# An FNet block with a gated MLP: a second scratch tile, two more tiles of statistics on VectorE, one load earlier, and the first products in another order

## The chip, the cores and the metric

The kernel runs on one core of one Trainium2 chip. The metric is the device time of one execution in microseconds (us). A core has five engines with an instruction queue each: TensorE (PE in the profile, its weight loads PEld), VectorE (DVE), ScalarE (ACT), GpSimd (POOL) and SyncE (SP, which here only issues DMAs). Each queue runs in order, and engines wait for each other through semaphores.

## The reference

```python
x = A_x                                              # 2048 x 512
mod = (silu(c) @ w_mod).reshape(1, 6, 1, 512)
sa, ca, ga, sb, cb, gb = mod[:, 0], ..., mod[:, 5]
h = layernorm(x) * (1 + ca) + sa
a = h @ dft_hid_re.T;  b = h @ dft_hid_im.T          # 512 x 512 each
x = x + ga * (dft_seq_re @ a - dft_seq_im @ b)       # 2048 x 2048 each
h = layernorm(x) * (1 + cb) + sb
z = gelu(h @ w_in);  z1, z2 = z[:, :896], layernorm(z[:, 896:])
g = w_sp @ z2 + b_sp[:, None]                        # w_sp 2048 x 2048
out = x + gb * ((z1 * g) @ w_out)
```

All in float32.

## The kernel before, in words

Every float32 product is made of three products in a faster format: a matrix is split into a rounded part (`..h`, a copy by ScalarE) and the rest (`..l`, a subtraction by VectorE), and `matmul3` adds hi x hi, lo x hi and hi x lo. A product of 128 x 128 by 128 x 512 is one matrix instruction.

Part A is computed with the sequence transform first: G = Cr h and Ci h, then G times the hidden matrices (`ht`). The sequence matrices come in *stages* of 512 x 512 (1 MB, four DMAs of 256 KB on SP's queue, two stage tiles). A stage is four *chunks* n of 128 rows. For a chunk, VectorE transposes 32 x 32 squares from the stage (`t`), ScalarE makes `ah` of it and VectorE `al`; TensorE then does 12 products, `gp` (four blocks k of h's columns, three products each). In the first quarter (t = 0, n = 0 to 31) chunks of Cr and Ci come in turn, four by four: chunks 0 to 3 and 8 to 11 are Cr, 4 to 7 and 12 to 15 are Ci, so that row tile s of x is first needed at chunk 0, 1, 2, 3, 8, 9 and so on: 16 tiles of 128 rows, `x0` to `x3` being the loads of four tiles each.

For a row tile s the normalized tile `xn` is split into `hh` and `hl`. Tiles 0 to 7 have their mean and variance from VectorE (`stats_x`: two small instructions, then a chain of three on POOL, `mvx`, `rsx`, `nmrx`). Tiles 8 to 15 have them from ScalarE: `sum_x`, then `square_x`, with POOL's small steps between (`sums`), each a pass over the tile. `norm_x` then applies them on ScalarE, and column 0 of the tile is set to 1 (by ScalarE for the first four tiles, by POOL for the others): the kernel folds the modulation (1 + ca, sa) into the hidden matrices instead, and needs its two rows of `mod` as columns over the partitions. For those, w_mod's blocks (`wb1`, `wb0`, 1 MB each) are transposed in squares by VectorE into a scratch tile `wt`, multiplied by silu(c) spread over the partitions (`crow`), and summed along the row by ScalarE into one column of `col1` or `col0`: `weigh_column(j, k)` and `sum_column(j, k)`, eight times. `wt` is one tile.

The order is written by hand. A loop over chunks n (*slots*) calls `prep(n)`, which issues t and ah of chunk n + 3 and al of chunk n + 2, then `mm_a(n)`, the products, then `run(n)`, whatever `at(n, ...)` put down for this slot. A load of x or w_mod that stands in a slot goes to SP's queue at that place; a stage is loaded when the last chunk of the stage before the last has been transposed. Ahead of the first slot, `keep_busy` gives TensorE products of no use (`busyp`) until data arrive.

After 32 chunks the sums are split (`gh`, `gl`), the second quarter follows, and the products with ht (`yp`) of the quarter before, their addition to x, the second norm and the stores stand in its slots. Then come z1, z2, the product with w_sp (`gw`) and with w_out.

Of the kernel before, what the change touches and what calls it, by code (L numbers as in the profile page):

```python
# [19 lines left out]
def fnet_gmlp_kernel(  # L20
# [24 lines left out]
    nc = tc.nc  # L45
    S, D = x.shape[1:]
# [11 lines left out]
    def pool(name, side="left", bufs=1):  # L58
        return tc.tile_pool(name=name, bufs=bufs, side=side, reuse_waits="tile")
# [11 lines left out]
    def bank(k, name):  # L71
        return psum.tile([P, 512], F32, tag=f"bank{k}", bufs=1, name=name)
# [5 lines left out]
    def split(hi, lo, src):  # L78

        nc.scalar.activation(hi, src, AF.Copy)  # L80
        nc.vector.tensor_tensor(lo, src, hi.bitcast(F32), op=ALU.subtract)

    def matmul3(acc, ah, al, bh, bl, first, last):
        nc.tensor.matmul(acc, ah, bh, start=first, stop=False)  # L84
        nc.tensor.matmul(acc, ah, bl, start=False, stop=False)  # L85
        nc.tensor.matmul(acc, al, bh, start=False, stop=last)  # L86
# [20 lines left out]
    def apply(dst, src, scale_shift):  # L107
        nc.scalar.activation(dst, src, AF.Identity, bias=scale_shift[1], scale=scale_shift[0])
# [3 lines left out]
    def at(n, f, *a):  # L112
        fill.setdefault(n, []).append((f, a))
# [14 lines left out]
    N2 = 4 * len(src)  # L128
# [17 lines left out]
    def squares(dst, block, k):  # L146
        nc.vector.transpose(dst.rearrange("p (b i) -> p b i", i=32), block[:, :, 32 * k:32 * k + 32])  # L147
# [36 lines left out]
    rows = p2.enter_context(pool("rows", "right"))  # L184
    s1 = ctx.enter_context(ExitStack())
    spool = s1.enter_context(pool("spool", "right"))
# [7 lines left out]
    ones = cpool.tile([P, P], F32, name="ones")  # L194
# [28 lines left out]
    WB, WT, COL = {}, {}, {}  # L223
# [13 lines left out]
        COL[j] = htpool.tile([P, ND], F32, name=f"col{j}")  # L237

    def weigh_column(j, k):
        WT[j, k] = spool.tile([P, D], F32, tag="wt", bufs=1, name=f"wt{j}_{k}")  # L240
        squares(WT[j, k], WB[j], k)
        nc.vector.tensor_tensor(WT[j, k], WT[j, k], WB["c"], op=ALU.mult)

# [11 lines left out]
    def keep_busy(n, k):  # L255

        ps = bank(k, "busyp")
        for _ in range(n):
            nc.tensor.matmul(ps, ones, busy, start=True, stop=True)
# [14 lines left out]
    X, XG, LN, NRM, h_hi, h_lo = {}, {}, {}, {}, {}, {}  # L274

    def load_x(g, ks=range(4)):

        if g not in XG:
            XG[g] = spool.tile([P, 4, D], F32, tag="x", bufs=2, name=f"x{g}")
        k0, k1 = ks[0], ks[-1] + 1  # L280
        v = x.rearrange("(g a k i) d -> g a i k d", g=NQ, a=4, i=32)
        for a in range(4):
            nc.sync.dma_start(XG[g][32 * a:32 * a + 32, k0:k1, :], v[g, a][:, k0:k1, :])
        for k in ks:
            X[4 * g + k] = XG[g][:, k, :]
# [17 lines left out]
        NRM[s] = m[:, 2:3], m[:, 3:4]  # L303

    def norm_x(s):
        if s not in LN:
            LN[s] = spool.tile([P, D], F32, tag="xn", bufs=4, name=f"xn{s}")
        apply(LN[s], X.pop(s), NRM.pop(s))
        if s < 4:
            nc.scalar.activation(LN[s][:, 0:1], ones[:, 0:1], AF.Copy)  # L310
        else:
            nc.gpsimd.memset(LN[s][:, 0:1], 1.0)

    def parts_h(s, t):

# [13 lines left out]
    GP, gt_hi, gt_lo, YP = {}, {}, {}, {}  # L329
# [3 lines left out]
    def mm_a(n):  # L333
        t, r = divmod(n, 8 * NQ)
        j, s = ((r // 4) % 2, r // 8 * 4 + r % 4) if t == 0 else (r // NS, r % NS)
        if s == 0:
            for k in range(ND):
                GP[t, j, k] = bank(4 * j + k if t == 0 else ring[0] % 6, f"gp{t}_{j}_{k}")
                ring[0] += t > 0
        ah, al = AH.pop(n), AL.pop(n)  # L340
        for k in range(ND):
            matmul3(GP[t, j, k], h_hi[s][:, k, :], h_lo[s][:, k, :], ah, al, s == 0, s == NS - 1)
        if s == NS - 1:
            for k in range(ND):
                ps = GP.pop((t, j, k))
                gt_hi[t, j, k] = GP_[0].tile([P, Q], F32R, tag=f"gh{j}_{k}", name=f"gh{t}_{j}_{k}")
                gt_lo[t, j, k] = GP_[0].tile([P, Q], F32R, tag=f"gl{j}_{k}", name=f"gl{t}_{j}_{k}")
                split(gt_hi[t, j, k], gt_lo[t, j, k], ps)
# [261 lines left out]
    load_x(0, range(2, 4))  # L610
    load(1)
    load_x(1, range(2))
    keep_busy(7, 5)
    for s in range(2):
        stats_x(s)
    for s in range(2):
        norm_x(s)
# [7 lines left out]
    lo_h(1)  # L625
    prep_lo(1)
    norm_x(2)
    prep_hi(2)
    stats_x(3)
    hi_h(2)  # L630
    norm_x(3)
    at(0, lo_h, 2)
    at(0, hi_h, 3)
# [3 lines left out]
    at(9, silu_row)  # L637
    at(4, load_x, 2)
    at(5, load_columns, 1)
    at(8, load_columns, 0)  # L640
    at(12, load_x, 3)
    at(19, load_ht, 0)
    at(28, load_ht, 1)
    for s, n in ((4, 4), (5, 4), (6, 6), (7, 6)):
        at(n, stats_x, s)
        at(n + 1, norm_x, s)
        at(n + 2, hi_h, s)
        at(n + 3, lo_h, s)
    for s, n in zip(range(8, NS), (10, 11, 12, 13, 18, 19, 20, 21)):
        at(n, sum_x, s)  # L650
        at(n + 1, square_x, s)
        at(n + 2, norm_x, s)
        at(n + 3, hi_h, s)
        at(n + 4, lo_h, s)
    for j, ns in ((1, (12, 13, 16, 18)), (0, (19, 20, 21, 23))):
        for k, n in enumerate(ns):
            at(n, weigh_column, j, k)
            at(n + 1, sum_column, j, k)
# [6 lines left out]
    ones_r = htpool.tile([P, P], F32R, name="ones_r")  # L665
    at(24, nc.scalar.activation, ones_r, ones, AF.Copy)
    at(26, change_pools)
    for j, turn, weigh, row, fold, hi in ((0, (24, 25, 26, 27), (29, 29, 30, 30), 25, (34, 34, 35, 36), (38, 35, 36, 37)),
                                          (1, (33, 38, 39, 40), (39, 40, 41, 41), 37, (44, 45, 46, 47), (48, 46, 47, 48))):
        for k in range(ND):  # L670
            at(turn[k], turn_ht, j, k)
            at(weigh[k], weigh_ht, j, k)
            at(fold[k], fold_ht, j, k)
        at(row, scale_w0, j)
        at(row + 1, store_w0, j)
        at(row + 5, load_w0, j)
# [14 lines left out]
    for t in range(NQ):  # L691
        n = 8 * NQ * (t + 1)
        for i in range(4):
            y = N2 - 1 if t == NQ - 1 else (54, 56, 58, 60)[i] if t == 0 else n + (8, 10, 12, 14)[i] if t == 1 else n + 1 + 3 * i
            if i < 2:
                at(y - 4, load_xr, t, i)
            if t == 0:
                at((41, 42, 43, 45)[i], mm_y, t, i, (0,))
                at((42, 43, 44, 46)[i], keep_y, t, i)
            at(y, mm_y, t, i, (0, 1) if t else (1,))  # L700
            if t < NQ - 1:
                at(y + 1, post_y, t, i)
                at(y + 2, norm_y, t, i)
                at(y + 3 if t else 71 + i, post_h, t, i)
                if i < 2:
                    at(y + 2 if t else y + 3, load_xr, t, i + 2)
            else:
                if i > 1:
                    at(N2 - 0.25, prep, N2 + i - 2)
                at(N2 - 0.25, post_y, t, i)  # L710
                at(N2 - 0.25, norm_y, t, i)
                at(N2 - 0.25, post_h, t, i)
                if i < 2:
                    at(N2 - 0.25, load_xr, t, i + 2)
# [59 lines left out]
    for t in range(NQ):  # L774
        n = N4 + NS * (t + 1)
# [14 lines left out]
    t = NQ - 1  # L790
# [61 lines left out]
```

## Time and profile before

| | |
|---|---|
| median of 3 runs | 1002.48 us (1002.38 to 1003.36) |
| the profiled execution | 1002.74 us |
| its span in the trace | 1000.9 us |
| granted TensorE clock, mean | 0.997 |
| TensorE busy | 989.3 us (99%), 4346 instructions |
| VectorE, ScalarE, GpSimd busy | 543.6, 315.1, 142.3 us |

All times of a trace count from the span's start. A row of the timeline has the start, the duration, the engine, the line of the code, the operation, what is written from what, and in brackets how long the engine was idle before and whose work ended the wait. A row of the waits has the engine and line that waited, whose work it waited for, the sum in us, how often, and the longest. The granted clock is the share of full speed that TensorE was given.

### The profile page before, as it was taken

What the parts mean: (1) busy time and instruction counts of PE and PEld (TensorE: products, weight loads), DVE (VectorE), ACT (ScalarE), POOL (GpSimd) and SP (SyncE); (2) the same over time, 40 slices, a digit from 0 to 9 for tenths busy, and PEclk for the clock granted to TensorE, in tenths of its full rate; (3) what the DMA queues carried; (4) which work ended last, traced back from release to release, by engine and by line L of the source; (5) the groups of instructions that cost most, each with busy time, mean ns of one, the idle gap of its engine ahead of it and who ended that gap; (6) DMA issues with size and microseconds to landing.
All of it is one profiled execution on the core that took longest, in us unless ns stands there. A gap on an engine that the chain in (4) does not pass through costs nothing.

```text
span 1000.9 us, 11701 instructions
## 1 busy us (share of the span) xinstructions
PE 989.3 (99%) x4346; PEld 818.9 (82%) x4346; DVE 543.6 (54%) x830; ACT 315.1 (31%) x513; POOL 142.3 (14%) x282
## 2 busy tenths in 40 slices
PE   8998999999999999999999999999999999999998
PEld 5886888888878888888888998888888888888886
DVE  6768957775566546547433576555332622262315
ACT  4666423232132312222543665431111111111101
POOL 2321000112420122004321111102000200020002
PEclk9999999999999999999999999999999999999999
DMA  9993852666435443556553232435225222522131
GB/s 214 215 198 67 167 138 63 158 166 171 126 103 118 93 109 104 117 127 163 189 204 117 43 80 47 116 69 147 70 63 156 55 64 64 158 64 52 43 137 43
DMA packets 149466, 115.08 MB, mean 115 GB/s; under 512 B 7200, under 2 KB 130080, under 8 KB 149408
## 3 DMA queue, kind: packets, MB, share of 16 engines
q1 hardware_dynamic: 142576, 93.87, 40.7%
q0 software_dynamic: 6304, 20.46, 5.8%
q8 instruction: 34, 0.56, 0.2%
q14 instruction: 24, 0.20, 0.1%
q10 hardware_dynamic: 528, 0.00, 0.0%
HBM read 94.37 MB, written 19.93 MB: 114 GB/s over the span
## 4 chain that ended last, share of the span: by engine, by line
PE 94%; DVE 2%; ACT 1%; DMA 1%; issue 1%; SPq 0%; DVEq 0%; ACTq 0%
PE gp L85 11%; PE gp L86 11%; PE gp L84 10%; PE gw L84 10%; PE gw L86 10%; PE gw L85 10%; PE yp L85 3%; PE yp L84 3%; PE yp L86 3%; PE z2p L85 3%; PE z2p L84 3%; PE z2p L86 3%; PE z1p L84 3%; PE z1p L85 3%; PE z1p L86 3%; PE op L86 2%
## 5 line engine op out<-in xcount | busy, mean ns | idle before, releaser
L170 ACT ACTIVATE ah<-t 128x512 fp32r<-128x512 f32 x224 | 141.5, 632 | 535.6 <-PE gw L86 214.9
L179 DVE TENSOR_TENSOR al<-t,ah 128x512 fp32r<-128x512 f32 x224 | 153.1, 683 | 274.6 <-PE gw L85 143.0
L85 PE MATMUL gp<-al,hh 128*128 128x512 f32 x512 | 201.6, 394 | 4.7 <-DVE al L179 4.7
L84 PE MATMUL gp<-ah,hh 128*128 128x512 f32 x512 | 200.8, 392 | 1.7 <-ACT ah L170 1.7
L86 PE MATMUL gp<-ah,hl 128*128 128x512 f32 x512 | 201.1, 393 | 0.0
L86 PE MATMUL gw<-ah,zl 128*128 128x512 f32 x448 | 174.5, 390 | 0.0
L84 PE MATMUL gw<-ah,zh 128*128 128x512 f32 x448 | 174.5, 389 | 0.0
L85 PE MATMUL gw<-al,zh 128*128 128x512 f32 x448 | 174.5, 389 | 0.0
L147 DVE STREAM_TRANSPOSE t<-stage 128x512 f32<-128x512 f32 x208 | 146.4, 704 | 5.6 <-DMA stage<-in_A_dft_seq_re_dram 2.8
L85 PEld LDWEIGHTS gp<-al,hh 128*128 128x128 f32 x512 | 96.8, 189 | 26.5 <-DVE al L179 6.3
L84 PEld LDWEIGHTS gp<-ah,hh 128*128 128x128 f32 x512 | 97.0, 189 | 23.2 <-ACT ah L170 2.5
L86 PEld LDWEIGHTS gp<-ah,hl 128*128 128x128 f32 x512 | 97.0, 189 | 20.8 <-DVE hl L325 0.4
L86 PEld LDWEIGHTS gw<-ah,zl 128*128 128x128 f32 x448 | 84.1, 188 | 17.5
L85 PEld LDWEIGHTS gw<-al,zh 128*128 128x128 f32 x448 | 84.2, 188 | 17.4
L84 PEld LDWEIGHTS gw<-ah,zh 128*128 128x128 f32 x448 | 84.1, 188 | 17.3
L569 POOL TENSOR_TENSOR u<-u,g 128x512 f32<-128x512 f32 x16 | 21.4, 1340 | 336.1 <-DVE g L567 336.1
L85 PE MATMUL yp<-htl,gh 128*128 128x512 f32 x128 | 51.1, 399 | 0.0
L84 PE MATMUL yp<-hth,gh 128*128 128x512 f32 x128 | 50.5, 394 | 0.0
L86 PE MATMUL yp<-hth,gl 128*128 128x512 f32 x128 | 50.2, 392 | 0.0
L85 PE MATMUL z2p<-wil,ah 128*128 128x448 f32 x128 | 46.8, 366 | 0.0
L84 PE MATMUL z2p<-wih,ah 128*128 128x448 f32 x128 | 46.8, 366 | 0.0
L86 PE MATMUL z2p<-wih,al 128*128 128x448 f32 x128 | 46.8, 366 | 0.0
(125 smaller groups left out, 1132.0 us busy)
## 6 DMA issues: line engine op xcount, KB each, us to landing
stage<-in_A_dft_seq_re_dram SPq DMA_DIRECT2D x64, 256.0 KB, 4.8
stage<-in_A_dft_seq_im_dram SPq DMA_DIRECT2D x64, 256.0 KB, 4.7
stage<-in_B_w_sp_dram SPq DMA_DIRECT2D x64, 256.0 KB, 4.9
stage<-h_d SPq DMA_DIRECT2D x32, 256.0 KB, 4.6
z_d<-z POOLq DMA_DIRECT2D x28, 256.0 KB, 5.9
u<-z_d SPq DMA_DIRECT2D x4, 1792.0 KB, 7.9
wm<-in_w_mod_dram SPq DMA_DIRECT2D x16, 256.0 KB, 5.7
xr<-in_A_x_dram POOLq DMA_DIRECT2D x16, 256.0 KB, 3.0
```

Of the source, the lines that this page charges most:

```text
L84: nc.tensor.matmul(acc, ah, bh, start=first, stop=False)
L85: nc.tensor.matmul(acc, ah, bl, start=False, stop=False)
L86: nc.tensor.matmul(acc, al, bh, start=False, stop=last)
L147: nc.vector.transpose(dst.rearrange("p (b i) -> p b i", i=32), block[:, :, 32 * k:32 * k + 32])
L170: nc.scalar.activation(AH[n], T[n], AF.Copy)
L179: nc.vector.tensor_tensor(AL[n], T.pop(n), AH[n].bitcast(F32), op=ALU.subtract)
L569: eng.tensor_tensor(U[t][:, f, :], U[t][:, f, :], g, op=ALU.mult)
```

## The change

Four kinds of edits, all in part A's first quarter but one. `weigh_column` takes a second scratch tile for even k, in the place of a row tile ("y") that is not used until later. Row tiles 8 and 9 have their statistics from VectorE instead of ScalarE, and the slots of tiles 8 to 15 and of the columns are set anew; the load of x3 stands in slot 8 and that of wb0 in slot 12. Column 0 of a normalized tile is set by POOL for all tiles, ahead of the norm, which then writes columns 1 to 511. The chunks 0 to 3 have their 12 products in the order hi x hi for the four blocks, lo of the chunk x hi for the four, hi x lo for the four, and there are eight products of no use ahead instead of seven. The one edit outside: the y products of the second quarter (t = 1) stand one slot earlier.

```diff
     def weigh_column(j, k):
-        WT[j, k] = spool.tile([P, D], F32, tag="wt", bufs=1, name=f"wt{j}_{k}")
+        pl, tag = (spool, "wt") if k % 2 else (rows, "y")
+        WT[j, k] = pl.tile([P, D], F32, tag=tag, bufs=1, name=f"wt{j}_{k}")
...
     def norm_x(s):
+
         if s not in LN:
             LN[s] = spool.tile([P, D], F32, tag="xn", bufs=4, name=f"xn{s}")
-        apply(LN[s], X.pop(s), NRM.pop(s))
-        if s < 4:
-            nc.scalar.activation(LN[s][:, 0:1], ones[:, 0:1], AF.Copy)
-        else:
-            nc.gpsimd.memset(LN[s][:, 0:1], 1.0)
+        nc.gpsimd.memset(LN[s][:, 0:1], 1.0)
+        apply(LN[s][:, 1:], X.pop(s)[:, 1:], NRM.pop(s))
...
         ah, al = AH.pop(n), AL.pop(n)
+        if n < 4:
+            for a, b in ((h_hi[s], ah), (h_hi[s], al), (h_lo[s], ah)):
+                for k in range(ND):
+                    nc.tensor.matmul(GP[0, 0, k], a[:, k, :], b, start=s == 0 and b is ah and a is h_hi[s], stop=False)
+            return
         for k in range(ND):
             matmul3(GP[t, j, k], h_hi[s][:, k, :], h_lo[s][:, k, :], ah, al, s == 0, s == NS - 1)
...
-    keep_busy(7, 5)
+    keep_busy(8, 5)
...
-    at(8, load_columns, 0)
-    at(12, load_x, 3)
+    at(8, load_x, 3)
+    at(12, load_columns, 0)
...
-    for s, n in ((4, 4), (5, 4), (6, 6), (7, 6)):
+    for s, n in ((4, 4), (5, 4), (6, 6), (7, 6), (8, 10), (9, 10)):
+        m = n + (s == 9)
         at(n, stats_x, s)
-        at(n + 1, norm_x, s)
...
+        at(m + 1, norm_x, s)
...
-    for s, n in zip(range(8, NS), (10, 11, 12, 13, 18, 19, 20, 21)):
+    for s, n in zip(range(10, NS), (11, 12, 15, 16, 18, 19)):
         at(n, sum_x, s)
...
-    for j, ns in ((1, (12, 13, 16, 18)), (0, (19, 20, 21, 23))):
+    for j, ns in ((1, (12, 14, 17, 18)), (0, (21, 22, 23, 24))):
         for k, n in enumerate(ns):
             at(n, weigh_column, j, k)
             at(n + 1, sum_column, j, k)
...
-    for j, turn, weigh, row, fold, hi in ((0, (24, 25, 26, 27), (29, 29, 30, 30), 25, (34, 34, 35, 36), (38, 35, 36, 37)),
+    for j, turn, weigh, row, fold, hi in ((0, (25, 26, 27, 28), (29, 29, 30, 30), 26, (34, 34, 35, 36), (38, 35, 36, 37)),
...
-            y = N2 - 1 if t == NQ - 1 else (54, 56, 58, 60)[i] if t == 0 else n + (8, 10, 12, 14)[i] if t == 1 else n + 1 + 3 * i
+            y = N2 - 1 if t == NQ - 1 else (54, 56, 58, 60)[i] if t == 0 else n + (7, 9, 11, 13)[i] if t == 1 else n + 1 + 3 * i
```

`sum_x`, `square_x`, `norm_x`, `hi_h` and `lo_h` of a tile stand in slots n to n + 4 as before. Line numbers shift a little: L242 becomes L243, L325 becomes L324, and products of chunks 0 to 3 have L343.

What the order of instructions becomes, at three places. First VectorE at the turns of chunks 24 and 25 (the number after a name's underscore tells buffers apart; `t24` is chunk 24's transpose). Before:

```order
L147 STREAM_TRANSPOSE wt0_1_840<-wb0_486 128x512
L242 TENSOR_TENSOR wt0_1_840<-wt0_1_840,crow_295 128x512
L251 TENSOR_SCALAR col1_388<-col1_388 128x4
L253 TENSOR_SCALAR col2_844<-col1_388 128x4
L147 STREAM_TRANSPOSE t24_846<-stage6_699 128x512
L179 TENSOR_TENSOR al23_850<-t23_806,ah23_808 128x512
L147 STREAM_TRANSPOSE wt0_2_877<-wb0_486 128x512
L242 TENSOR_TENSOR wt0_2_877<-wt0_2_877,crow_295 128x512
L147 STREAM_TRANSPOSE t25_880<-stage6_699 128x512
L179 TENSOR_TENSOR al24_884<-t24_846,ah24_848 128x512
L325 TENSOR_TENSOR hl12_898<-xn12_764,hh12_864 128x512
```

VectorE in the changed kernel, the same chunks:

```order
L252 TENSOR_SCALAR col1_389<-col1_389 128x4
L254 TENSOR_SCALAR col2_866<-col1_389 128x4
L147 STREAM_TRANSPOSE t24_868<-stage6_712 128x512
L179 TENSOR_TENSOR al23_872<-t23_834,ah23_836 128x512
L147 STREAM_TRANSPOSE wt0_0_890<-wb0_603 128x512
L243 TENSOR_TENSOR wt0_0_890<-wt0_0_890,crow_296 128x512
L147 STREAM_TRANSPOSE t25_893<-stage6_712 128x512
L179 TENSOR_TENSOR al24_897<-t24_868,ah24_870 128x512
L324 TENSOR_TENSOR hl14_911<-xn14_790,hh14_886 128x512
```

And ScalarE at the same turns, before:

```order
L170 ACTIVATE ah24_848<-t24_846 128x512
L320 ACTIVATE hh12_864<-xn12_764 128x512
L108 ACTIVATE xn13_798<-x3_590,sums13_799 128x512
L299 ACTIVATE xn14_835,sums14_836<-x3_590,sums14_836 128x512
L294 ACTIVATE xn15_872,sums15_873<-x3_590 128x512
L247 ACTIVATE wt0_1_840,col0_491<-wt0_1_840 128x512
L170 ACTIVATE ah25_882<-t25_880 128x512
L320 ACTIVATE hh13_900<-xn13_798 128x512
```

ScalarE in the changed kernel:

```order
L170 ACTIVATE ah24_870<-t24_868 128x512
L319 ACTIVATE hh14_886<-xn14_790 128x512
L108 ACTIVATE xn15_829<-x3_487,sums15_830 128x511
L170 ACTIVATE ah25_895<-t25_893 128x512
L319 ACTIVATE hh15_913<-xn15_829 128x512
L248 ACTIVATE wt0_0_890,col0_608<-wt0_0_890 128x512
L170 ACTIVATE ah26_921<-t26_919 128x512
L248 ACTIVATE wt0_1_916,col0_608<-wt0_1_916 128x512
```

What moved: at chunk 24 the third weighing of column 0 stood on VectorE, now it is the first, the others follow in the next three slots; on ScalarE the passes over x that stood ahead of the column's sum are done by then, and tile 14 is split where tile 12 was.

Second, TensorE's first products, before:

```order
L259 MATMUL busyp_139<-busy_111,ones_105 128x512 x7
L84 MATMUL gp0_0_0_233<-ah0_175,hh0_171 128x512
L85 MATMUL gp0_0_0_233<-al0_179,hh0_171 128x512
L86 MATMUL gp0_0_0_233<-ah0_175,hl0_177 128x512
L84 MATMUL gp0_0_1_234<-ah0_175,hh0_171 128x512
L85 MATMUL gp0_0_1_234<-al0_179,hh0_171 128x512
```

TensorE's first products in the changed kernel:

```order
L260 MATMUL busyp_139<-busy_111,ones_105 128x512 x8
L343 MATMUL gp0_0_0_234<-ah0_176,hh0_172 128x512
L343 MATMUL gp0_0_1_235<-ah0_176,hh0_172 128x512
L343 MATMUL gp0_0_2_236<-ah0_176,hh0_172 128x512
L343 MATMUL gp0_0_3_237<-ah0_176,hh0_172 128x512
L343 MATMUL gp0_0_0_234<-al0_180,hh0_172 128x512
```

The first product that needs `al0` is now the fifth, not the second, and one product of no use more stands ahead.

Third, SP's queue of loads, before (four DMAs a row; `hraw` is a hidden matrix):

```order
L139 DMA stage4_467<-in_A_dft_seq_re_dram 32x16x128 x4
L139 DMA wb0_486<-in_w_mod_dram 32x16x128 x4
L139 DMA stage5_571<-in_A_dft_seq_im_dram 32x16x128 x4
L283 DMA x3_590<-in_A_x_dram 32x4x512 x4
L139 DMA stage6_699<-in_A_dft_seq_re_dram 32x16x128 x4
```

SP's queue in the changed kernel:

```order
L139 DMA stage4_468<-in_A_dft_seq_re_dram 32x16x128 x4
L284 DMA x3_487<-in_A_x_dram 32x4x512 x4
L139 DMA stage5_584<-in_A_dft_seq_im_dram 32x16x128 x4
L139 DMA wb0_603<-in_w_mod_dram 32x16x128 x4
L139 DMA stage6_712<-in_A_dft_seq_re_dram 32x16x128 x4
```

The last group of x and column 0's block of w_mod have changed places, stage 5 between them.

More of the change, by code (lines that the diff above doesn't have):

```diff
@@ L639, in fnet_gmlp_kernel @@
     at(5, load_columns, 1)
-    at(8, load_columns, 0)
-    at(12, load_x, 3)
+    at(8, load_x, 3)
+    at(12, load_columns, 0)
     at(19, load_ht, 0)
     at(28, load_ht, 1)
-    for s, n in ((4, 4), (5, 4), (6, 6), (7, 6)):
+    for s, n in ((4, 4), (5, 4), (6, 6), (7, 6), (8, 10), (9, 10)):
+        m = n + (s == 9)
         at(n, stats_x, s)
-        at(n + 1, norm_x, s)
-        at(n + 2, hi_h, s)
-        at(n + 3, lo_h, s)
-    for s, n in zip(range(8, NS), (10, 11, 12, 13, 18, 19, 20, 21)):
+        at(m + 1, norm_x, s)
+        at(m + 2, hi_h, s)
+        at(m + 3, lo_h, s)
+    for s, n in zip(range(10, NS), (11, 12, 15, 16, 18, 19)):
         at(n, sum_x, s)
```

## The prediction

> **What bounds the kernel now.** I read the page's first part, then TensorE's waits, then the clock in windows around those waits, and last the timeline of the two places where TensorE stood still.
>
> ```profile
> span 1000.9 us, 11701 instructions
> PE 989.3 (99%) x4346; PEld 818.9 (82%) x4346; DVE 543.6 (54%) x830; ACT 315.1 (31%) x513; POOL 142.3 (14%) x282
> ```
> ```profile
> PE gp L85 <- DVE al L179: 4.7, 4, 3.0
> PE gp L84 <- ACT ah L170: 1.7, 1, 1.7
> ```
>
> TensorE (PE) is busy all but 11.6 us of the span, and no edit takes a product away, so only idle time and slow clock can be won. Its waits (us in total, times, longest) for the two splits of a chunk, ah and al, are 6.4 us. Each busy microsecond can still be a slow one, so I cut windows where the granted clock changes (length, then busy time of PE, PEld, DVE, ACT and POOL, then the clock):
>
> ```profile
> 8.72:12.13 3.41, 1.48 (x5) 0.34 (x3) 2.09 (x4) 2.69 (x5) 0.13 (x1) 1.00 1.12 238
> 12.13:15.55 3.42, 3.42 (x8) 2.73 (x9) 3.39 (x7) 0.76 (x2) 1.68 (x3) 0.50 1.24 222
> 76.98:80.39 3.41, 2.73 (x12) 2.18 (x12) 0.62 (x2) 3.27 (x8) 0.64 (x3) 1.00 0.01 2
> 80.39:83.81 3.42, 0.47 (x3) 0.18 (x1) 2.83 (x5) 1.23 (x4) 0.55 (x3) 1.00 0.00 0
> 83.81:87.22 3.41, 3.41 (x8) 2.41 (x9) 3.05 (x6) 3.41 (x9) 1.12 (x4) 0.50 0.00 0
> ```
>
> Twice the clock is at 0.50 for 3.41 us, and both times the 3.41 us before were mostly idle: 1.48 of 3.41 busy (43%), and 0.47 (14%). The window that was 2.73 busy (80%) kept its clock. Each slow window does half a window's work: 1.7 us lost.
>
> **The middle stall.** Rows of VectorE, ScalarE and TensorE at 76 to 84 us:
>
> ```profile
> 76.32 0.71 DVE L147 STREAM_TRANSPOSE t<-stage 128x512 f32<-128x512 f32 x1
> ...
> 80.94 0.71 DVE L147 STREAM_TRANSPOSE wt<-wb 128x512 f32<-128x512 f32 x1 [3.34 <-ACT wt L247]
> 81.69 0.69 DVE L242 TENSOR_TENSOR wt<-wt,crow 128x512 f32<-128x512 f32 x1
> 82.30 0.70 DVE L147 STREAM_TRANSPOSE t<-stage 128x512 f32<-128x512 f32 x1
> 82.93 0.65 DVE L179 TENSOR_TENSOR al<-t,ah 128x512 fp32r<-128x512 f32 x1
> ```
> ```profile
> 78.18 0.80 ACT L108 ACTIVATE xn<-x,sums 128x512 f32<-128x512 f32 x1
> ...
> 80.20 0.61 ACT L247 ACTIVATE wt<-wt 128x512 f32<-128x512 f32 x1
> ```
> ```profile
> 77.66 0.50 PE L85 MATMUL gp<-al,hh 128*128 128x512 f32 x1 [1.15 <-DVE al L179]
> ...
> 83.63 0.66 PE L85 MATMUL gp<-al,hh 128*128 128x512 f32 x1 [2.95 <-DVE al L179]
> ```
>
> The t rows are the transposes of chunks 24 and 25: 5.98 us apart, where TensorE eats a chunk (12 products at 0.227 us, from the last two rows of the start below) in 2.72 us. The reason stands between them: VectorE's next wt transpose waits 3.34 us for ScalarE's sum of the previous wt (there is one such tile), and that sum is the last of ScalarE's passes of the turn, which began only when this turn's t was there. VectorE and ScalarE so take turns. TensorE's lead (al is made two chunks ahead, 5.4 us) is used up, and it stands 1.15 us, then 2.95 us, then runs 3.41 us at half clock: 1.15 + 2.95 + 1.7 = 5.8 us.
>
> **Scratch, stats and x's last group: -5.8.** With two wt tiles a weighing waits for the sum of two weighings ago, which ScalarE has behind it while VectorE does the turn between. A turn is then as long as its work on one engine: VectorE, by the distances of the starts at 80.94 to 82.93, has 0.75 + 0.61 + 0.63 for wt and t, and about 0.6 each for al and hl: 3.2 us. ScalarE has norm, square and sum of x in the 2.0 us from 78.18 to 80.20, the column sum at 0.6 and two splits at about 0.6 each: 3.8 us in the fullest slots of before. After the change no slot holds all six (three of x, the column sum, ah and hh): the column-0 sums stand in slots 22 to 25, where no square, sum or normalizing of x is left behind slot 21. So a turn is 3.2 us at most, and four in a row (21 to 24) lose 4 x 0.5 = 2 us of a lead of 5.4: no stall. The stats of tiles 8 and 9 on VectorE add two passes of 0.67 us (row below) and two small ones to slot 10, under 2 us, again inside the lead, and take two sums and two squares, 2.6 us, from ScalarE. Their short POOL chains wait for nobody in the products' path.
>
> ```profile
> L92 DVE BATCH_NORM_STATS2 bstx<-x 128x6 f32<-128x512 f32 x8 | 5.4, 674 | 4.3 <-DMA x<-in_A_x_dram 4.0 <-issue 0.2
> ```
>
> On SP's queue x3 and wb0 change places, stage 5 between them; each is 1 MB, so stages 5 and 6 have as many bytes ahead of them as before.
>
> ```profile
> wb<-in_w_mod_dram SPq DMA_DIRECT2D x8, 256.0 KB, 9.0
> ```
> ```profile
> 40.90 4.54 SPq L139 DMA_DIRECT2D wb<-in_w_mod_dram  x4
> 45.53 5.23 SPq L139 DMA_DIRECT2D stage<-in_A_dft_seq_im_dram  x4
> 50.86 2.93 SPq L283 DMA_DIRECT2D x<-in_A_x_dram  x4
> ```
>
> In wb0's old place x3 is there at about 45.4 + 9.0 = 54.4, and the first sum of it, slot 15, is due when TensorE starts chunk 15: 24.44 + 11 x 2.72 - 1.5 = 52.9. ScalarE may wait 1.5 us there, with ah split three chunks (8.2 us) ahead behind it: hidden. wb0 lands at about 53.8 + 9.0 = 62.8; slot 21 is at 69. If it were late, VectorE would stand with the next t and al behind the weighing, TensorE two chunks later. What follows from column 0 moves by one slot (the turn of ht, its scaled row); the next step that needs it, the fold of ht, stays at slot 34, eight slots on. The first ht tile takes the row tile "y" at slot 25, after the sum at 24 of the weighing that holds it: at most one ScalarE pass, 0.6 us.
>
> **The start: -1.5.**
>
> ```profile
> 8.20 0.19 PEld L259 LDWEIGHTS busyp<-busy,ones 128*128 128x128 f32 x1 [0.24 <-issue]
> 8.63 0.19 PEld L259 LDWEIGHTS busyp<-busy,ones 128*128 128x128 f32 x1 [0.24 <-issue]
> ```
> ```profile
> 11.35 0.49 PE L84 MATMUL gp<-ah,hh 128*128 128x512 f32 x1 [1.70 <-ACT ah L170]
> 12.07 0.77 PE L85 MATMUL gp<-al,hh 128*128 128x512 f32 x1 [0.23 <-DVE al L179]
> ...
> 16.28 0.39 PE L84 MATMUL gp<-ah,hh 128*128 128x512 f32 x1
> ...
> 24.44 0.39 PE L84 MATMUL gp<-ah,hh 128*128 128x512 f32 x1
> ```
> ```profile
> 13.92 0.69 DVE L179 TENSOR_TENSOR al<-t,ah 128x512 fp32r<-128x512 f32 x1
> ```
> ```profile
> 16.27 0.20 ACT L310 ACTIVATE xn<-ones 128x1 f32<-128x1 f32 x1
> 16.38 0.62 ACT L170 ACTIVATE ah<-t 128x512 fp32r<-128x512 f32 x1
> 16.90 0.62 ACT L320 ACTIVATE hh<-xn 128x512 fp32r<-128x512 f32 x1
> ...
> 19.89 0.61 ACT L320 ACTIVATE hh<-xn 128x512 fp32r<-128x512 f32 x1
> ```
>
> The rows of TensorE at 16.28 and 24.44 are products 13 and 49: 8.16 / 36 = 0.227 us each at full clock. The warm-up's products show two loads each, 0.43 apart; the eighth adds 0.86, so they end at 10.5, and the gap ahead of the first real product shrinks from 1.70 to 0.84 (its ah is not moved: VectorE's transpose waits for the stage, not for the norm). Nor does al, due at 12.07, stop anything now: four products with ah alone come first, until 11.35 + 0.91 = 12.26. The window 8.72:12.13 is then busy for 1.48 + 0.86 + 0.23 = 2.57 of 3.41, 75%. The rows bound the answer, 43% lost the clock and 80% kept it; 75% is nearest to 80%, so I take full clock. Then chunk 0 ends at 11.35 + 12 x 0.227 = 14.07; chunk 1 has its al (13.92 + 0.69 = 14.61) before its fifth product (14.98), and ends at 16.8. Now hh binds: chunk 2's ends at 17.52 in the rows, about 0.25 earlier without ScalarE's small write at 16.27, which goes to POOL, ahead of the norm. Chunk 2 runs 17.3 to 20.0, chunk 3 from 20.25 (hh 20.50 less 0.25) to 22.97. Before, chunk 4 began at 24.44: 1.5 us won. With half the clock until 15.55: 3.4 products by 12.13, 8.0 in the slow window, chunk 0 done at 15.7, chunk 4 at 23.85: 0.6 won.
>
> A page of the Trainium skill, TensorE: Matmul & The Clock Gate, Part 1, says the clock halves after at least one idle window of about 3.4 us, and that the windows run free of the kernel's start. The window length agrees with the rows (3.41); that it takes an idle window does not, since 43% busy was enough. By the page's rule the start stays at full clock, 994.8; by the row at 43%, were the line above 75%, it is 995.7. And if the windows fall elsewhere in another execution, the worst one holds the whole 0.84 us gap, 75% again.
>
> **The second quarter: -0.4.**
>
> The waits for al are four: 0.23, 1.15 and 2.95 stand in the rows above, and 0.37 of the 4.7 is left. That one lies where VectorE has the split of a finished sum and a row block's y work together in one slot, in A's second quarter. The y products and their work stand one slot earlier now, so I count the 0.4 as won; the bounds are 0.4 lost and 0.4 won, since the next split could be met the same way.
>
> **The sum.** The profiled execution took 1002.74 us, 1.84 more than its span; the median of the three runs is 0.26 below it. Off come 5.8 + 1.5 + 0.4 = 7.7 us: 995.0 for the profiled execution, and 994.8 against the median, which I predict. All later work only starts earlier. Its own range, with the start between 0.6 and 2.2 (no hh wait) and 0.4 either way, is 994 to 996.5.
>
> **Rivals.** (1) The start stays cold: 994.8 + 0.9 = 995.7. For it: nothing between 43% and 80% was seen. (2) A rest of the middle stall stays, since VectorE's 3.2 us a turn is still above 2.72 and four weighings stand in a row: the smaller stall alone gives 996.0, the larger with its slow window 994.8 + 4.65 = 999.5. Against it: 2 of 5.4 us of lead used. (3) The change does not do what it says: two tiles, but ScalarE's sums stay late enough that every weighing still waits, and only 1.9 is won at the start and in the second quarter: 1000.6. Against it: it needs sums two slots late. (4) Slower: x3's load needs the buffer of x's second group and stands ahead of stage 5 in SP's queue. If it is held there, stage 5, wb0 and stage 6 are all late. Stage 5 lands near 50.8 + 5 = 56 and TensorE wants its first chunk at 24.44 + 16 x 2.72 - 1.5 = 66.5, so a hold past 10 us stops TensorE one for one, and past 20 us the kernel is over 1004.5. Against it: the normalizing of tile 7 that frees the buffer stands in slot 7, over when chunk 8 begins or little later (24.44 + 4 x 2.72 = 35.3), and the load's place on the queue comes at 40.9.
>
> **Chances.** Forecast 0.68, rival 1 0.17, rival 2 0.10, rival 3 0.03, rival 4 0.02. The range leaves out the larger stall, rivals 3 and 4 and a few unnamed tenths below: 993.6 to 997.4. About 0.2% (2.0 us) is what a measurement of this kernel tells from no change: faster 0.95, same 0.03, slower 0.02.
>
> **What would show it.** Right: no wait of TensorE for al between 60 and 110 us, a clock of 1.00 from 12 us on, VectorE's wt rows with no idle time put down to ScalarE's sum, chunk 4 of the first sum near 23 us, and chunk 24 near 77.4. Wrong: a window at 0.50 after 12 us (rival 1), one after 70 us (2), wt rows that still wait (3), a t that waits for stage 5 (4), or new idle time further on, where I count none.

## The result, and the profile after

The changed kernel takes 994.18 us (median of four executions, 994.08 to 994.25), the kernel before 1002.43 us in the same comparison (1000.97 to 1003.36): 8.25 us less, ratio 0.9919 with a 95% interval of 0.9902 to 0.9936. The profiled execution took 994.23 us, 8.51 us less than that of before.

The page's first part and the whole list of TensorE's waits, after:

```profile
span 992.5 us, 11713 instructions
PE 986.3 (99%) x4348; PEld 816.7 (82%) x4348; DVE 545.6 (55%) x834; ACT 311.9 (31%) x501; POOL 145.9 (15%) x284
```
```profile
PE busyp L260 <- DVE busy L201: 1.5, 1, 1.5
PE gp L343 <- ACT ah L170: 0.7, 1, 0.7
PE gp L343 <- ACT hh L319: 0.2, 1, 0.2
```

No wait for al is left; of the 6.4 us for ah and al, 0.7 us stays, ahead of the first useful product. The two windows that ran at 0.50 before (length, then busy time of PE, PEld, DVE, ACT and POOL, then the clock) are at full clock.

```profile
12.13:15.55 3.42, 3.42 (x16) 2.81 (x15) 3.38 (x8) 0.63 (x1) 1.61 (x3) 1.00 1.25 222
...
83.81:87.22 3.41, 3.41 (x17) 2.83 (x16) 1.84 (x3) 1.88 (x4) 1.10 (x2) 1.00 0.15 25
```

VectorE's transposes into wt, by groups over the first 140 us, before and then after: the last column is the idle time ahead of them and its releaser. It was all ScalarE's sum of the tile, and it is gone.

```profile
L147 DVE STREAM_TRANSPOSE wt<-wb 128x512 f32<-128x512 f32 x8 | 5.7, 708 | 11.9 <-ACT wt L247 11.9
```
```profile
L147 DVE STREAM_TRANSPOSE wt<-wb 128x512 f32<-128x512 f32 x8 | 5.6, 704 | 0.0
```

Where the 8.4 us of the span lie is read from the starts of the same products in both. Chunk 4 after (its row before, at 24.44, stands in the prediction):

```profile
11.58 1.20 PE L343 MATMUL gp<-ah,hh 128*128 128x512 f32 x4 [0.73 <-ACT ah L170]
...
17.56 1.19 PE L343 MATMUL gp<-ah,hh 128*128 128x512 f32 x4 [0.25 <-ACT hh L319]
...
23.17 0.39 PE L84 MATMUL gp<-ah,hh 128*128 128x512 f32 x1
```

The first products behind the first quarter (qp) and the last of the modulation rows at the second quarter's end (modp), before and then after, with first and last start:

```profile
L393 PE MATMUL qp<-sacc,ones_r x2: 390/390/390, 118.0 to 151.5; 128*128 128x512 f32 x2
...
L270 PE MATMUL modp<-ws,ones_r x4: 394/394/395, 179.3 to 313.4; 128*128 128x512 f32 x4
```
```profile
L397 PE MATMUL qp<-sacc,ones_r x2: 390/390/390, 110.2 to 143.7; 128*128 128x512 f32 x2
...
L271 PE MATMUL modp<-ws,ones_r x4: 394/394/394, 171.6 to 304.9; 128*128 128x512 f32 x4
```

Chunk 4 comes 1.27 us earlier (the start), qp 7.8 (so the middle gave 6.5), the last modp 8.5 (so the second quarter gave 0.7). Behind that the distance stays; the end of the span is 8.4 us earlier.

### The profile page after: what moved, and what is told of

Its sections match the earlier page's. It is cut to its first block, busy times and chain, and to the rows that moved or that the text cites. A ratio compares the mean times of both kernels' runs of the same rounds, so it can differ in the third digit from the quotient of the medians.

```text
span 992.5 us, 11713 instructions
## 1 busy us (share of the span) xinstructions
PE 986.3 (99%) x4348; PEld 816.7 (82%) x4348; DVE 545.6 (55%) x834; ACT 311.9 (31%) x501; POOL 145.9 (15%) x284
## 4 chain that ended last, share of the span: by engine, by line
PE 98%; DMA 1%; DVE 0%; SPq 0%; ACT 0%; issue 0%; POOL 0%
PE gp L84 11%; PE gp L85 11%; PE gp L86 11%; PE gw L86 10%; PE gw L85 10%; PE gw L84 10%; PE yp L85 3%; PE yp L84 3%; PE yp L86 3%; PE z2p L84 3%; PE z2p L85 3%; PE z2p L86 3%; PE z1p L84 3%; PE z1p L86 3%; PE z1p L85 3%; PE op L85 2%
## 5 line engine op out<-in xcount | busy, mean ns | idle before, releaser
L84 PE MATMUL gp<-ah,hh 128*128 128x512 f32 x496 | 193.3, 390 | 0.0
L85 PE MATMUL gp<-al,hh 128*128 128x512 f32 x496 | 193.3, 390 | 0.0
L86 PE MATMUL gp<-ah,hl 128*128 128x512 f32 x496 | 193.2, 389 | 0.0
L84 PEld LDWEIGHTS gp<-ah,hh 128*128 128x128 f32 x496 | 93.1, 188 | 19.9
L86 PEld LDWEIGHTS gp<-ah,hl 128*128 128x128 f32 x496 | 93.1, 188 | 19.6
L85 PEld LDWEIGHTS gp<-al,hh 128*128 128x128 f32 x496 | 93.1, 188 | 19.5
```

## The experiments

Times are medians in us, the ratio is to the kernel before in the same comparison, with its 95% interval; before's median was 1002.48 for the first four, 1002.55 for the next four, 1002.94 for the last four. The last column is the mean granted clock of each execution: one window of 3.41 us at half clock takes 0.0017 off it, so an execution that lost one is at 0.998 or below. A mean of 0.999 comes from half clock behind the last product: in e3's profiled execution it is the last 1.63 us of the span, 0.0008.

| kernel | edit | time | ratio | clock of the executions |
|---|---|---|---|---|
| e1 | changed, one wt tile | 994.83 (994.60 to 994.89) | 0.9922 [0.9907, 0.9937] | 0.999 to 1.000 |
| e2 | before, with two wt tiles | 996.37 (995.66 to 996.58) | 0.9939 [0.9922, 0.9955] | 1.000, three times 0.998 |
| e3 | changed, old load order | 996.81 (996.37 to 997.31) | 0.9942 [0.9928, 0.9957] | 0.999 to 1.000 |
| e4 | changed, tiles 8 and 9 on ScalarE | 994.27 (994.25 to 994.35) | 0.9917 [0.9902, 0.9932] | 0.999 to 1.000 |
| e5 | changed, seven products of no use | 994.37 (994.10 to 995.01) | 0.9919 [0.9904, 0.9934] | three times 1.000, 0.998 |
| e6 | changed, old order of first products | 994.58 (994.46 to 994.85) | 0.9921 [0.9906, 0.9935] | 1.000 |
| e7 | changed, old norm_x | 994.62 (994.37 to 994.66) | 0.9921 [0.9904, 0.9937] | 1.000 |
| e8 | changed, old y slots | 994.95 (994.88 to 995.12) | 0.9924 [0.9909, 0.9939] | 0.999 to 1.000 |
| e9 | e1 and e3 together | 1001.45 (1001.02 to 1002.16) | 0.9987 [0.9978, 0.9996] | 0.996 to 1.000 |
| e10 | e1 and e4 together | 994.73 (994.37 to 994.80) | 0.9921 [0.9907, 0.9936] | 1.000 |
| e11 | changed, five products of no use | 994.62 (994.16 to 995.13) | 0.9921 [0.9906, 0.9936] | 0.998, 1.000, 0.998, 0.999 |
| e12 | changed, all edits of the start undone | 996.44 (995.83 to 997.04) | 0.9941 [0.9924, 0.9957] | twice 0.998, twice 0.996 |

### The middle: one tile or two, x early or late (e1, e2, e3, e9)

**e1**, the changed kernel with one scratch tile:

```diff
-        pl, tag = (spool, "wt") if k % 2 else (rows, "y")
-        WT[j, k] = pl.tile([P, D], F32, tag=tag, bufs=1, name=f"wt{j}_{k}")
+        WT[j, k] = spool.tile([P, D], F32, tag="wt", bufs=1, name=f"wt{j}_{k}")
```

> The changed kernel with one scratch tile wt again; slots, loads and all else as changed. Theory 1 (the prediction's: the second tile removes the middle stall): the wait of VectorE's wt rows for ScalarE's sum is back, TensorE stands near 75 and 80 us and has a slow window, 5.8 to 6.5 us come back, about 1000.3. Theory 2 (the new slots remove it: in slots 22 to 25 nothing but ah, hh and the column's sum is on ScalarE, so that a turn with one tile is t 0.7, ah 0.5, hh 0.5, sum 0.7, wt 0.75 + 0.6, some 3.8 us, and four of them use 4.3 of the 5.4 us of lead): wt rows wait for the sum again, but TensorE does not, 994.2.

It took 994.83 us: the middle stall stays away with one tile. VectorE does wait again (5.0 us in all, where the kernel before had 11.9), and still TensorE has no wait for al. VectorE, and then ScalarE, in e1:

```profile
64.73 0.71 DVE L147 STREAM_TRANSPOSE wt<-wb 128x512 f32<-128x512 f32 x1 [2.58 <-ACT wt L247]
...
79.69 0.71 DVE L147 STREAM_TRANSPOSE wt<-wb 128x512 f32<-128x512 f32 x1 [0.20 <-ACT wt L247]
```
```profile
78.41 0.63 ACT L170 ACTIVATE ah<-t 128x512 fp32r<-128x512 f32 x1 [2.19 <-DVE t L147]
78.95 0.62 ACT L247 ACTIVATE wt<-wt 128x512 f32<-128x512 f32 x1
79.47 0.19 ACT L247 ACTIVATION_READ_ACCUMULATOR wt<-wt 128x1 f32 x1
81.84 0.63 ACT L170 ACTIVATE ah<-t 128x512 fp32r<-128x512 f32 x1 [2.19 <-DVE t L147]
```

The engines take turns as before, but for the last columns ScalarE has only ah and the column sum in its turn. A chunk then takes 3.43 us (ah at 78.41 and 81.84), 0.7 more than TensorE's 2.72, for the few chunks that have a column: the lead of two chunks pays for that. One turn still has a norm and a sum of x ahead of the column sum; its wait, 2.58 us at 64.73, is the longest of e1, and the lead pays for that too.

**e2**, the opposite: the kernel before with the second tile and nothing else.

```diff
-        WT[j, k] = spool.tile([P, D], F32, tag="wt", bufs=1, name=f"wt{j}_{k}")
+        pl, tag = (spool, "wt") if k % 2 else (rows, "y")
+        WT[j, k] = pl.tile([P, D], F32, tag=tag, bufs=1, name=f"wt{j}_{k}")
```

> The kernel before with the second scratch tile and nothing else. Theory 1: no wait of wt for the sum, the middle stall is gone, 5.8 to 6.5 us below before (1002.4): about 996.3; the start's slow window is still there. Theory 2: the tile alone does not help, since ScalarE's passes of slots 18 to 21 (3.8 us a turn) still make it late: 1000 to 1002.4. Both could be right of their own edit: then this gives 996.3 and the one-tile kernel 994.2.

996.37 us, and of the waits for al only two of 0.6 us in all are left, none of them in the middle. Its one execution at clock 1.000 took 995.66, the three at 0.998 took 996.20 to 996.58. So the tile alone removes the middle stall as well, with the old slots and the old order of loads. The 995.66 us are 1.5 over the changed kernel, about what undoing the edits e6, e7 and e8 below costs together (1.6): with the second tile there, the new slots and loads of the middle win nothing that can be seen.

**e3**, the changed kernel with the two loads in their old order:

```diff
-    at(8, load_x, 3)
-    at(12, load_columns, 0)
+    at(8, load_columns, 0)
+    at(12, load_x, 3)
```

> The changed kernel with wb0 loaded in slot 8 and x3 in slot 12, as before, the first sum of x3's tiles still in slot 15. Theory A (the load's place matters once tiles 12 to 15 have their sums three slots earlier): x3 lands at about 62 us, ScalarE stands with the sum of tile 12 from about 53 to 62, ah of chunk 19 behind it; TensorE wants that at 63.5, so it stops 1 to 3 us near 64, perhaps with a slow window: 995.5 to 998.5. Rival (the lead of three chunks hides it): 994.2.

996.81 us, 2.6 more than the changed kernel. In the profiled executions it is 2.1 (996.37 against 994.23), all of it ahead of qp (112.4 against 110.2). SP's queue, changed kernel and then e3, and ScalarE in e3:

```profile
41.01 2.50 SPq L284 DMA_DIRECT2D x<-in_A_x_dram  x4
```
```profile
50.71 2.95 SPq L284 DMA_DIRECT2D x<-in_A_x_dram  x4
```
```profile
61.95 0.63 ACT L295 ACTIVATE xn<-x 128x512 f32<-128x512 f32 x1 [6.97 <-DMA x<-in_A_x_dram]
```

x's last group is issued 9.7 us later, and ScalarE, which has its sum in slot 15 now, stands 6.97 us with everything queued behind it. The lead that is lost there is missing later: between starts of products 0.3 to 0.6 us is lost at 64, 75 and 84 us (0.23 us of it shown as a wait), and smaller bits behind.

**e9**, both: one tile and the old order of loads, all slots new.

```diff
-        pl, tag = (spool, "wt") if k % 2 else (rows, "y")
-        WT[j, k] = pl.tile([P, D], F32, tag=tag, bufs=1, name=f"wt{j}_{k}")
+        WT[j, k] = spool.tile([P, D], F32, tag="wt", bufs=1, name=f"wt{j}_{k}")
...
-    at(8, load_x, 3)
-    at(12, load_columns, 0)
+    at(8, load_columns, 0)
+    at(12, load_x, 3)
```

> The changed kernel with one tile for the columns and, besides, w_mod's first half loaded ahead of x's last group, as before (slots new). By themselves the first cost 0.65 us and the second 2.6 us. Theory 1 (one tile does harm only where ScalarE's steps for x's tiles 12 to 15 fall on the same chunks as the column sums; late tiles bring them together again): TensorE's long waits for al near chunks 24 to 26 are back, 1 to 3 us each, with them slow windows of the clock in some executions: 998.5 to 1001. Theory 2 (the two add): 997.2 to 997.8, with no wait for al over 0.6 us.

1001.45 us, 7.3 over the changed kernel, where 0.65 and 2.6 would add to 3.25. The stall is back. VectorE, ScalarE and TensorE in e9:

```profile
71.26 0.71 DVE L147 STREAM_TRANSPOSE wt<-wb 128x512 f32<-128x512 f32 x1 [3.70 <-ACT wt L247]
```
```profile
62.44 0.63 ACT L294 ACTIVATE xn<-x 128x512 f32<-128x512 f32 x1 [7.10 <-DMA x<-in_A_x_dram]
...
67.18 0.71 ACT L299 ACTIVATE xn<-x,sums 128x512 f32<-128x512 f32 x1
67.79 0.19 ACT L299 ACTIVATION_READ_ACCUMULATOR xn<-x,sums 128x1 f32 x1
67.88 0.62 ACT L170 ACTIVATE ah<-t 128x512 fp32r<-128x512 f32 x1
68.40 0.61 ACT L318 ACTIVATE hh<-xn 128x512 fp32r<-128x512 f32 x1
69.19 0.81 ACT L108 ACTIVATE xn<-x,sums 128x511 f32<-128x511 f32 x1 [0.17 <-POOL xn L309]
69.91 0.62 ACT L294 ACTIVATE xn<-x 128x512 f32<-128x512 f32 x1
70.43 0.19 ACT L294 ACTIVATION_READ_ACCUMULATOR xn<-x 128x1 f32 x1
70.52 0.61 ACT L247 ACTIVATE wt<-wt 128x512 f32<-128x512 f32 x1
```
```profile
73.94 0.80 PE L85 MATMUL gp<-al,hh 128*128 128x512 f32 x1 [3.13 <-DVE al L179]
```

VectorE could have gone on at 67.5, and waits 3.70 us for the column sum at 70.52, because ScalarE has ah, hh and three passes over x's tiles ahead of it. TensorE then stands 3.13 us for al. In e1 the lead paid for the longest such wait, 2.58 us. In e9 ScalarE had first stood 7.10 us for x's last group, and TensorE met an al that was not ready at 65.07 us already: no lead was left.

So the stall needs both: one tile, which makes VectorE wait for the column sum, and x's passes late, which takes the lead and puts more of them ahead of the column sums. The second tile takes the first away, the earlier load with the new slots the second. Late passes alone cost 2.6 us (e3) and one tile alone 0.65, so 4.0 of the 7.3 come only with both. How much of that is the lost lead and how much the fuller turns was not told apart. The slow clock is not what it costs: three of e9's ten executions had a mean clock of 1.000 and took 1001.35 to 1001.56 us, the six at 0.998 took 1001.02 to 1002.16.

### Statistics on VectorE (e4, e10)

**e4**, tiles 8 and 9 by sum and square on ScalarE, as before:

```diff
-    for s, n in ((4, 4), (5, 4), (6, 6), (7, 6), (8, 10), (9, 10)):
+    for s, n in ((4, 4), (5, 4), (6, 6), (7, 6)):
...
-    for s, n in zip(range(10, NS), (11, 12, 15, 16, 18, 19)):
+    for s, n in zip(range(8, NS), (9, 10, 11, 12, 15, 16, 18, 19)):
```

> The changed kernel with the statistics of tiles 8 and 9 by sum and square on ScalarE again, in slots 9 to 11. Theory A (moving them took a load from ScalarE that counts): ScalarE's turns of slots 10 to 12 are 2.6 us longer in all, the weighings come later, and some of the middle stall comes back, 0.5 us or more: 994.7 to 997. Rival (the lead hides 2.6 us, since ScalarE is idle between the ahs there): 994.2.

994.27 us, no difference. **e10** has the same edit and one tile:

```diff
-        pl, tag = (spool, "wt") if k % 2 else (rows, "y")
-        WT[j, k] = pl.tile([P, D], F32, tag=tag, bufs=1, name=f"wt{j}_{k}")
+        WT[j, k] = spool.tile([P, D], F32, tag="wt", bufs=1, name=f"wt{j}_{k}")
...
-    for s, n in ((4, 4), (5, 4), (6, 6), (7, 6), (8, 10), (9, 10)):
+    for s, n in ((4, 4), (5, 4), (6, 6), (7, 6)):
```

> The changed kernel with one tile for the columns and, besides, tiles 8 and 9 summed and squared by ScalarE. By themselves the first cost 0.65 us, the second 0.1 us. Theory 1 (the same as for the late tiles: 8 and 9 are done by chunk 13, long before the column sums of chunks 21 to 24): 994.6 to 995.0. Theory 2 (statistics on VectorE are what spares the one tile): the waits for al are back, 997 or more.

994.73 us, as e1 (994.83). These statistics neither cost nor save anything, with two tiles or one.

### The start (e5, e6, e7, e11, e12)

**e5** and **e11** undo the eighth product of no use, or three of them:

```diff
-    keep_busy(8, 5)
+    keep_busy(7, 5)
```

In e11 the new line is `keep_busy(5, 5)`.

> The changed kernel with seven products of no use at the start where it has eight; all else as changed. Theory 1 (the prediction's: the clock's window must be kept busy enough): the pause before the first useful product grows by one such product, from 0.73 us to some 1.3 us, the window that holds it is then some 55 to 65% busy, between the 43% that lost the clock before and the 76% that kept it; in some executions, by where the window falls, the mean clock is 0.998 and the time 994.8 to 995.3, in the others 1.000 and 994.2. Theory 2 (the eighth product does nothing, chunk 2 waits for its hh anyway): 994.1 to 994.3 in every execution, clock 1.000.

> The changed kernel with five products of no use at the start in place of eight. Theory 1 (clock): TensorE stands still for 3 us or more ahead of the first useful product, the window after it runs at half clock in every execution, mean clock 0.998, 994.8 to 995.3 (the one such execution with seven products took 995.01). Theory 2 (the start is bound by hh at chunk 2 whatever the clock): 994.1 to 994.4 even at clock 0.998.

Three executions of e5 kept the clock and took 994.10 to 994.39; the one at 0.998 took 995.01. Of e11, two took 994.16 and 994.24 at full clock, two 995.00 and 995.13 at 0.998. A lost window at the start so costs 0.6 to 0.9 us, and the eighth product is an insurance against it, worth nothing in an execution that keeps the clock. The changed kernel, e1, e3, e4, e6, e7, e8 and e10 have eight products, and none of their 32 executions lost a window. That two executions of e11 kept it was expected by neither theory. In e11's profiled execution, which lost it, the windows cut where the clock changes are:

```profile
7.97:11.38 3.41, 0.00 (x0) 0.00 (x0) 1.29 (x2) 2.61 (x5) 0.92 (x5) 1.00 1.12 240
11.38:14.79 3.41, 3.39 (x8) 2.71 (x9) 3.37 (x7) 1.12 (x2) 1.13 (x2) 0.50 1.24 232
```

**e6**, the first products in the old order:

```diff
-        if n < 4:
-            for a, b in ((h_hi[s], ah), (h_hi[s], al), (h_lo[s], ah)):
...
-            return
```

> The changed kernel with the products of the first four chunks in the old order (hh, al, hl products per column block instead of all hh products first). Theory 1: TensorE meets chunk 0's al and chunk 1's al before they are ready, loses 0.5 us at the second product (as the kernel with only the second tile did, from 11.47 to 12.20) and again at chunk 1; not all is taken back: 994.5 to 994.9. Theory 2 (hh of chunk 2 sets the time): what is lost at chunk 0 comes off the 0.4 us wait at chunk 2: 994.2 to 994.3.

994.58 us, 0.40 more. The second product waits for al again:

```profile
12.36 0.50 PE L85 MATMUL gp<-al,hh 128*128 128x512 f32 x1 [0.22 <-DVE al L179]
```

**e7**, column 0 set by ScalarE behind the norm for the first four tiles:

```diff
-        nc.gpsimd.memset(LN[s][:, 0:1], 1.0)
-        apply(LN[s][:, 1:], X.pop(s)[:, 1:], NRM.pop(s))
+        apply(LN[s], X.pop(s), NRM.pop(s))
+        if s < 4:
+            nc.scalar.activation(LN[s][:, 0:1], ones[:, 0:1], AF.Copy)
+        else:
+            nc.gpsimd.memset(LN[s][:, 0:1], 1.0)
```

> The changed kernel with the first column of ones written by ScalarE for the first four tiles, behind the normalization of a full-width tile, as before. Theory 1: ScalarE's turn per tile is longer by one small step, hh of chunks 2 and 3 comes 0.25 to 0.5 us later, and TensorE's wait for hh at chunk 2 (now 0.25 us shown, 0.4 us between product starts) grows by that: 994.4 to 994.8. Theory 2: ScalarE waits for data there and the step fits into the wait: 994.2.

994.62 us, 0.44 more; the wait for hh at chunk 2 is 0.48 us, where the changed kernel has 0.25. The first product happened to begin at 11.26 us in this execution, 0.32 earlier than in the changed kernel's profiled one, and chunk 4 began at 23.31, 0.14 later: 0.46 us longer from the one to the other.

```profile
17.48 0.74 PE L346 MATMUL gp<-ah,hh 128*128 128x512 f32 x2 [0.48 <-ACT hh L322]
```

**e12** undoes all three edits of the start, those of e6 and e7 and

```diff
-    keep_busy(8, 5)
+    keep_busy(7, 5)
```

> The changed kernel with all three edits of the start undone (order of the first products, normalization, seven products of no use). Theory 1 (they add): 0.4 and 0.44 us, 995.0 in an execution at full clock, 0.65 to 0.9 more, 995.6 to 995.9, in one that loses a window. Theory 2 (one wait behind the other, they do not add): 994.6 to 994.8 at full clock.

No execution of it kept the full clock. The two at 0.998 took 995.83 and 996.01: 994.18 and 0.40 and 0.44 and e11's 0.87 (995.00 and 995.13 less 994.16 and 994.24, means) are 995.89, so the three add. The two at 0.996 lost a second window and took 996.88 and 997.04, which I had not expected. The profiled execution, one of the former, cut at its own changes of clock:

```profile
10.46:13.87 3.41, 1.87 (x8) 1.30 (x8) 3.25 (x7) 2.20 (x4) 0.00 (x0) 1.00 1.19 217
13.87:17.28 3.41, 3.41 (x10) 2.64 (x9) 3.19 (x7) 1.36 (x3) 2.28 (x5) 0.50 1.19 229
```

### The second quarter (e8)

```diff
-            y = ... else n + (7, 9, 11, 13)[i] if t == 1 else ...
+            y = ... else n + (8, 10, 12, 14)[i] if t == 1 else ...
```

> The changed kernel with the second quarter's y products in their old slots, one later each. Theory 1: the wait of TensorE for al in the second quarter is back (0.37 us shown before, some 0.55 us between product starts, and smaller hiccups with it): 994.6 to 994.95. Theory 2: the 0.75 us that the second quarter gave came with the shift of what lies around it and not with the slots: 994.2.

994.95 us, 0.77 more. The wait of before is back, in the same place of the second quarter; before and then e8:

```profile
290.92 0.39 PE L84 MATMUL gp<-ah,hh 128*128 128x512 f32 x1
291.69 0.50 PE L85 MATMUL gp<-al,hh 128*128 128x512 f32 x1 [0.38 <-DVE al L179]
292.04 0.40 PE L86 MATMUL gp<-ah,hl 128*128 128x512 f32 x1
```
```profile
283.13 0.39 PE L84 MATMUL gp<-ah,hh 128*128 128x512 f32 x1
283.91 0.50 PE L85 MATMUL gp<-al,hh 128*128 128x512 f32 x1 [0.38 <-DVE al L179]
```

## Why the prediction was right, and where a step was off

The forecast was 994.8 us; it came to 994.18. By the profiled executions, 7.7 us was predicted and 8.5 came.

- **The middle: 5.8 predicted, 6.5 measured.** The mechanism was right as far as VectorE's wait for the column sum goes (e9 brings the stall back by it, with a lead that a late load has used up), its size was read too small. I added the idle times that the rows show. Those count from the modelled end of the product before, which lasts 0.39 us, while products start 0.227 us apart. By starts in the kernel before:

```profile
76.12 0.39 PE L84 MATMUL gp<-ah,hh 128*128 128x512 f32 x1
...
77.99 0.39 PE L86 MATMUL gp<-ah,hl 128*128 128x512 f32 x1
...
80.29 0.39 PE L84 MATMUL gp<-ah,hh 128*128 128x512 f32 x1
...
84.23 0.80 PE L86 MATMUL gp<-ah,hl 128*128 128x512 f32 x1
84.83 0.63 PE L84 MATMUL gp<-ah,hh 128*128 128x512 f32 x1
...
87.32 0.40 PE L84 MATMUL gp<-ah,hh 128*128 128x512 f32 x1
```

  From 76.12 to the product at 77.66 are 1.54 us, 1.31 lost (shown: 1.15), and the next one, at 77.99, is 0.1 late; from 80.29 to 83.63 are 3.34, 3.11 lost (shown: 2.95); from 83.63 to 87.32 stand eight starts, 3.69 less 8 x 0.227, 1.87 lost (taken: 1.7). That is 6.4 of the 6.5; the rest I did not find in one place.
- **What removes it.** The prediction gave two reasons in one breath: two tiles, and no turn with all six passes of ScalarE. It did not see that either is enough. e1 and e2 show it, and e9 that without both 7.3 us is lost, 2.6 of which the late load costs with two tiles too.
- **x3 and wb0 on SP's queue: nothing.** Right for the change: x's tile 12 is summed at 54.91 us with no wait, where I had it there at 54.4. But that the step cost nothing did not make it idle: with the new slots, the old order costs 2.6 us (e3). The prediction priced only the new order.
- **A turn of 3.2 us at most.** In the changed kernel VectorE's transposes of t start at 71.41, 74.73 and 77.88 us, 3.32 and 3.15 apart, and no wait for al follows. Rival 2 did not come.
- **Statistics: nothing.** Right (e4, e10).
- **The start: 1.5 predicted, 1.27 measured.** The clock was kept, as predicted; the first product began at 11.58 instead of 11.35, since the first transpose of the stage began 0.23 us later in this execution (10.15 against 9.92 us). hh binds at chunk 2, 0.25 us, as the arithmetic had it (17.56 against 17.3). The three edits come to 0.40, 0.44 and, where a window would be lost, 0.87: 1.7 in such an execution.
- **The gap ahead of the first useful product: 0.84 predicted, at worst a window 75% busy.** In the changed kernel's profiled execution it was 0.73, and its window, 9.41 to 12.82 us, was 2.68 of 3.41 busy (79%). But the gap is not the same in every execution: with the same eight products it was 0.20 us in e8 and 1.45 in e9. These products' weight loads come 0.85 us apart at first and 0.43 later, and the pace changed between 4.2 and 5.0 us in e9, between 6.8 and 7.3 in e8; the prediction used the later pace alone and one place of the change. So the worst such window in the traces was 59% busy (e9, below). It kept the clock too, but the prediction had not reckoned with it, and that part of the kept clock was luck.
- **Rival 1, the start cold: 0.9 more.** The price was right (0.6 to 0.9 in e5, 0.87 in e11). The rule of the Trainium skill that I weighed (TensorE: Matmul & The Clock Gate, Part 1: the clock halves after an idle window) covers the window of e11 that was 0.00 busy; it does not cover e12's, which was 1.87 of 3.41 busy (55%) and was followed by half clock too, as the 43% of before was.
- **The second quarter: 0.4 predicted, 0.7 measured.** The same reading error: 0.38 us is shown, but from 290.92 to 291.69 are 0.77 us, 0.54 lost, and the next product starts 0.35 us later instead of 0.227, 0.12 more: 0.66. The doubt whether the next split would be met the same way (0.4 either way) was for nothing: no wait is left there.

Of the 27 executions of the kernel before in the experiments' comparisons, 25 had a mean clock of 0.996 to 0.998 and took 1002.13 us or more; two had 1.000 and took 1000.93 and 1001.09. By the clock those 25 had lost one window or two. The lost windows, 3.4 us by the profile of an execution with two, are so worth some 1.9 us between executions (the median of the 25 is 1002.87). Why not 3.4 was not tried; at the start part of a lost window is time that TensorE would have waited for hh. The changed kernel's executions lie within 0.17 us, those of before within 2.6.

## What to carry to other kernels

Two engines that hand one scratch tile to each other run in series. The price is small while the consumer's lead covers it, and it becomes a stall when other passes of the slower engine fill the same turns and the lead is used up. Here either a second tile, or new slots with an earlier load, removed the stall, and trying each part alone tells which edits can be left out. Price a wait of a pipelined engine by the distance between starts less the usual pitch, not by the idle time shown. Before work is put into earlier slots, see that its load is issued earlier too.

## What the runs showed of the hardware

- The clock is lost without a whole idle window. Ahead of or between products, windows that were 0%, 14%, 32% (e9, 69.71 to 73.13, below), 43% and 55% busy were followed by one at 0.50. Windows of 59% (e9, 8.29 to 11.70), 61% (e10, 8.26 to 11.67), 66% (e2, 10.50 to 13.91) and 80% kept it. In e9 a window that was itself at half clock and 2.60 of 3.41 busy (76%) was followed by a second one at half clock. Since 59% at full clock was enough to keep it, 76% is not too little by itself: either time at half clock counts for less, or getting the clock back asks for more than keeping it. The busy share is a rough measure of what counts: behind the last products of e10 a window of 43% (987.88 to 991.30) was followed by one at full clock. The profile gives each product 0.39 us, though they start 0.227 apart in a row, so scattered products make a window look busier than the same number in a row.

```profile
8.29:11.70 3.41, 2.00 (x5) 0.57 (x3) 1.29 (x2) 2.38 (x5) 0.80 (x4) 1.00 1.12 223
...
69.71:73.13 3.42, 1.10 (x5) 0.56 (x3) 1.84 (x3) 1.52 (x5) 0.19 (x1) 1.00 0.02 5
73.13:76.54 3.41, 2.60 (x6) 2.12 (x7) 3.18 (x7) 3.13 (x9) 1.11 (x2) 0.50 1.08 249
76.54:79.95 3.41, 3.41 (x9) 2.65 (x9) 3.33 (x7) 3.03 (x6) 1.79 (x6) 0.50 1.24 214
```

- That does not explain everything: two of four executions of e11 kept the full clock (994.16 and 994.24 us), though its pause in the profiled execution, 3.85 us, leaves every placing of windows one that is at most 44% busy. These two executions have no profile, so their pauses are not known, and this stays open.
- A small step of GpSimd on one column takes 0.27 us or 1.09 us; in the long one VectorE subtracts (al from 17.02 and hl from 17.63 us) nearly all the while. The norm of tile 3 waits for it (it starts at 18.40), and its hh, done at 20.26, comes just ahead of chunk 3's first product at 20.42. GpSimd's spans are rough, and no run took the subtractions away.

```profile
15.35 0.27 POOL L104 TENSOR_SCALAR nmrx<-mvx,rsx 128x1 f32<-128x1 f32 x1
...
17.27 1.09 POOL L104 TENSOR_SCALAR nmrx<-mvx,rsx 128x1 f32<-128x1 f32 x1
```
